# Two attention and feed-forward layers on one core: products with v leave the chip unnormalised, rows are divided per unit

## Chip, core and metric

The kernel runs on one core of a Trainium2 chip. Its engines are TensorE (PE, with PEld for its weight loads), VectorE (DVE), ScalarE (ACT), GpSimd (POOL) and SyncE (SP, which issues most transfers); sixteen DMA engines move the data. The metric is the device time of one execution in microseconds, less is better, told as the median of several runs.

## What is computed

The input is x, 2048 rows of 640 numbers in f32. Two layers are run with the same weights, each an attention block and a feed-forward block with layer normalisation in front and the input added behind:

```python
H = 32; Dh = D // H; W = 256            # D = 640, Dh = 20
q, k, v = split(layernorm(x) @ wqkv)    # 32 heads of 20
scores = q @ k.T * Dh ** -0.5           # key not after the query, under 256 rows back
x = x + concat_heads(softmax(scores) @ v) @ wo
h = relu(layernorm(x) @ w1 + b1) ** 2   # F = 1536
x = x + h @ w2 + b2
```

## The kernel before

**Units.** The rows are cut into units of T = 256 rows, eight a layer, so that the two layers make NU = 16 units (u = 0 to 15; u = 8 begins the second layer). A unit sees its own keys and those of the unit before. Numbers that enter dense products are held as two f16 tiles, a high part and what the rounding left, and `mm3` (L149) makes each product of three f16 products.

**Attention of a unit.** The 32 heads are handled in NQ = 8 quads of four. `max_quad` (PE L313, DVE L327) makes masked scores and their row maxima; `max_out` transposes four quads' maxima on PE (L335), splits them (L338, L339) and writes them by SP transfers (L346) into two spare rows of the q tile, so that the later score product already subtracts them. `exp_quad` makes the scores again (L365), takes exponentials on ACT (L372) and masks them on POOL (L383, L387). `pv_quad` multiplies with v (L412). Each head's v has a 21st column of the constant 1/64, so row 20 of each head's product is the sum of its exponentials, scaled. Before the change `pv_quad` then divides at once: the product is copied from PSUM on ACT (L423), transposed in 32x32 blocks on DVE (L426), the sums are inverted (L428), spread by a second transpose (L429), multiplied on POOL (L430), and split into f16 high and low parts (L433, L434). After every second quad four SP transfers (L438) write both parts to a DRAM tile `o`, 20 rows for each head.

**Dense stages.** `stage_qk` makes q (j = 0) and k (j = 1), five chunks of 128 columns each, copied out by ACT L243 and DVE L244, and sends them through DRAM (L249, L251, L259) into another layout. `stage_v` follows (L271). `load_o(u)` brings the attention output back (L450) and loads the rows of x to be added (L454). `stage_o` multiplies by wo, adds x (L465) and normalises the result. `y_cross` transposes by DMA (L217), `stage_y` on PE (L173). `stage_f` is the feed-forward block (L500 to L520). All accumulators, the transposes and the product with v share two PSUM buffers of the tag "mm".

**Order.** PE's order is the order of the program text; the other engines' orders are chosen by a planner. Generators yield a modelled cost in ns after each piece, and `together` runs a unit's quads and hands out pieces of the `dense` generator between them: a `share` of a modelled `cost` is spread evenly over the unit's quads, and with `whole` the rest is run at the unit's end. Maxima are made LEAD = 5 quads ahead of the exponentials. During unit u the dense work is q and k of u + 1, output product of u - 1, v of u + 1, feed-forward of u - 1. Unit 0 has q, k, v of unit 2 instead (a fifth of it is left for unit 1), units 1 and 15 have no projection of a next unit, and behind unit 15 come its output product and feed-forward as a tail. `load_o(u - 1)` is issued in unit u behind the scores of its first quad. The weights wo, w1 and w2 are loaded during units 0 and before (`load_w`, `late`): ACT issues each transfer (L118), makes the high part (L122), scales the rest (L124), and POOL makes the low part (L125).

## Time and profile before

| | us |
|---|---|
| median of three runs | 1797.43 |
| the three runs | 1800.69, 1797.43, 1793.38 |
| profiled execution | 1793.71 |
| its span | 1792.0 |

| engine | busy us | share of the span |
|---|---|---|
| PE | 1616.1 | 90% |
| PEld | 1177.0 | 66% |
| DVE | 1068.6 | 60% |
| ACT | 781.2 | 44% |
| POOL | 742.0 | 41% |

Times inside the profile count from the start of the span. L12 is line 12 of the kernel. An engine's idle time is put down to the instruction that ended it. A group of instructions is shown as line, engine, operation, output and input with their sizes, count, busy time and mean duration. Of the chain of waits that ended last, followed back from the end, 53% lie on PE, 19% on DVE, 8% on issuing, 8% on POOL, 6% on ACT and 5% on transfers. The mean granted clock of PE is 0.979.

### The profile page before, as it was taken

The numbers are of one execution on the slowest core, as the hardware profiler recorded it, in microseconds if no ns is written. First come the engines' busy times: TensorE is split into PE (matmuls) and PEld (weight loads), VectorE is DVE, ScalarE is ACT, GpSimd is POOL, SyncE is SP. The second block draws the span as 40 slices with busy tenths as digits, with TensorE's granted clock in tenths as the row PEclk, the third lists the DMA queues.
The fourth block names the chain that finished last, engine by engine and source line by source line (L and its number), as shares of the span: only waits on it lengthen the run. The fifth ranks groups of instructions, "written<-read, shape, count | busy, mean of one in ns | idle before, by whom it ended". The sixth has DMA issues, their size and how long they took to land.

```text
span 1792.0 us, 45770 instructions
## 1 busy us (share of the span) xinstructions
PE 1616.1 (90%) x17542; PEld 1177.0 (66%) x17542; DVE 1068.6 (60%) x3473; ACT 781.2 (44%) x1716; POOL 742.0 (41%) x1434
## 2 busy tenths in 40 slices
PE   5767798999999999999999999999999999998798
PEld 4544566676667766666777767667676767775567
DVE  6546465666666566666557665666656566564531
ACT  5464343444445344444535244453534435352522
POOL 4354343534435353443525244352534435353522
PEclk9889899999999999999999999999999999998999
DMA  6754103234161422515242432514143152511010
GB/s 207 182 162 115 39 24 109 59 90 112 35 141 46 119 65 76 126 35 139 48 131 57 112 86 63 135 38 126 46 108 90 53 131 45 134 27 61 17 37 30
DMA packets 239067, 154.90 MB, mean 86 GB/s; under 512 B 80640, under 2 KB 219776, under 8 KB 238848
## 3 DMA queue, kind: packets, MB, share of 16 engines
q1 hardware_dynamic: 230432, 142.46, 31.9%
q10 hardware_dynamic: 8416, 9.51, 1.9%
q8 instruction: 138, 2.26, 0.5%
q14 instruction: 81, 0.66, 0.1%
HBM read 82.58 MB, written 52.43 MB: 75 GB/s over the span
## 4 chain that ended last, share of the span: by engine, by line
PE 53%; DVE 19%; issue 8%; POOL 8%; ACT 6%; DMA 5%; SPq 1%; ACTq 0%; DVEq 0%; POOLq 0%
PE acc L149 41%; DVE bb L327 8%; PE pv L412 4%; ACT pt L372 4%; PE bb L365 3%; DVE mx L327 3%; PE bb L313 3%; POOL pt L387 2%; POOL pt L383 2%; DVE hh L505 2%; POOL r L503 2%; DMA qk<-qd 1%; DVE rb L426 1%; POOL po L430 1%; DVE qd L244 1%
## 5 line engine op out<-in xcount | busy, mean ns | idle before, releaser
L327 DVE CUSTOM_DVE_ANT_0 bb<-bb,maskb 128x384 f32<-128x384 f32 (+2 forms) x1024 | 512.6, 558 | 126.4 <-PE bb L313 125.3
L372 ACT ACTIVATE pt<-bb 128x512 f32<-128x512 f32 x736 | 372.1, 600 | 64.9 <-PE bb L365 63.9
L430 POOL TENSOR_TENSOR po<-po,rb 128x256 f32<-128x256 f32 x128 | 101.1, 790 | 651.2 <-DVE rb L429 544.8
L149 PE MATMUL acc<-y,w_s 128*128 128x256 f16 x2880 | 337.4, 275 | 13.5 <-ACT r L500 8.5
L149 PEld LDWEIGHTS <-w_s 128*128 128x128 f16 x2880 | 278.1, 98 | 75.0 <-issue 38.6
L149 PE MATMUL acc<-w_s,hh 128*128 128x320 f16 x2304 | 325.7, 299 | 0.0
L149 PE MATMUL acc<-yT,wq_s 128*128 128x256 f16 x2400 | 286.5, 278 | 14.8 <-DVE qd L244 9.8
L149 PEld LDWEIGHTS <-hh 128*128 128x128 f16 x2304 | 222.0, 98 | 97.0 <-issue 14.5
L149 PEld LDWEIGHTS <-wq_s 128*128 128x128 f16 x2400 | 233.9, 100 | 67.1 <-issue 35.9
L383 POOL TENSOR_SCALAR_AFFINE_SELECT pt<-pt 128x256 f32<-128x256 f32 x448 | 194.8, 443 | 100.4 <-ACT pt L372 89.0
L423 ACT COPY po<-pv 128x256 f32<-128x256 f32 x128 | 47.6, 372 | 379.3 <-PE pv L412 376.4
L412 PE MATMUL pv<-pt,vt 128*32 128x128 f32 (+1 forms) x3840 | 194.2, 332 | 20.1 <-ACT r L500 10.5
L387 POOL TENSOR_SCALAR_AFFINE_SELECT pt<-pt 128x256 f32<-128x256 f32 x512 | 202.4, 418 | 9.5 <-ACT pt L372 8.7
L505 DVE TENSOR_TENSOR hh<-r,hh 128x256 f16<-128x256 f32 x192 | 93.6, 499 | 137.0 <-ACT hh L504 133.2
L149 PE MATMUL acc<-wo_s,od 128*128 128x320 f16 x960 | 143.2, 305 | 32.4 <-DMA od<-o 17.0
L503 POOL TENSOR_TENSOR r<-r 128x256 f32<-128x256 f32 x192 | 116.9, 625 | 115.5 <-ACT r L500 114.3
L149 PE MATMUL acc<-wq_s,yT 128*128 128x320 f16 x960 | 142.9, 300 | 16.3 <-DVE mT L339 14.7
L412 PEld LDWEIGHTS pv<-pt,vt 128*32 128x32 f32 x3840 | 107.9, 110 | 70.9 <-issue 28.2
L433 ACT CAST ot<-po 128x256 f16<-128x256 f32 x128 | 52.3, 408 | 228.9 <-POOL po L430 228.9
L149 PEld LDWEIGHTS <-od 128*128 128x128 f16 x960 | 92.5, 99 | 81.2 <-issue 28.0
L327 DVE DVE_READ_ACCUMULATOR2_ANT mx<- 128x1 f32 x1024 | 143.6, 140 | 0.0
L365 PE MATMUL bb<-qt,kt 62*128 62x128 f16 (+1 forms) x1920 | 108.3, 246 | 27.9 <-DVE mx L327 20.2
(62 smaller groups left out, 1408.0 us busy)
## 6 DMA issues: line engine op xcount, KB each, us to landing
qk<-qd SPq DMA_DIRECT2D x32, 640.0 KB
qt<-qk SPq DMA_DIRECT2D x32, 480.0 KB
kt<-qk SPq DMA_DIRECT2D x32, 480.0 KB
qk<-qd SPq DMA_DIRECT2D x32, 320.0 KB
o<-ot SPq DMA_DIRECT2D x256, 40.0 KB
od<-o SPq DMA_DIRECT2D x32, 320.0 KB
stg<-in_B_w_dram ACTq DMA_DIRECT2D x30, 256.0 KB
xt<-in_A_x_dram SPq DMA_DIRECT2D x16, 320.0 KB
```

The costliest lines, as they stand in the source:

```text
L149: nc.tensor.matmul(acc, lhs(a, c), rhs(b, c), start=(k == 0), stop=(k == 3 * nk - 1))
L313: apart(nc.tensor.matmul(to, qt[r, p, i * P:(i + 1) * P], kt[r, p, a:b], start=True, stop=True), read)
L327: read.append(nc.vector.tensor_tensor_reduce(out=v, in0=v, in1=mask, scale=1.0, scalar=-3.0e38, op0=ALU.add, op1=ALU.max, accum_out=accum))
L365: apart(nc.tensor.matmul(bb[e][:, k, o:o + w], kt[r, 2 * qd + j, ko:ko + P], qt[r, 2 * qd + j, q0 * P:q0 * P + w], start=True, stop=True), ...
L372: at[0] = nc.scalar.activation(pt[:, :o], bb[e][:, k, :o], AF.Exp, scale=SCALE / (QS * QS))
L383: nc.gpsimd.affine_select(out=m, in_=m, pattern=[[0, 2], [-1, P]], compare_op=ALU.is_gt, fill=0.0, base=0, channel_multiplier=1)
L387: nc.gpsimd.affine_select(out=m, in_=m, pattern=[[0, 2], [1, P]], compare_op=ALU.is_ge, fill=0.0, base=0, channel_multiplier=-1)
L412: nc.tensor.matmul(pv[32 * jj:32 * (jj + 1), q0 * P:(q0 + qn) * P], vf[:, c:c + 32], pj[:, j, :], start=(k == 0), stop=(k == len(steps) - ...
L430: nc.gpsimd.tensor_tensor(po, po, rb.rearrange("p a b -> p (a b)"), op=ALU.mult)
L433: nc.scalar.copy(oh, pf)
L503: nc.gpsimd.tensor_tensor(r, r, r, op=ALU.mult)
L505: nc.vector.tensor_sub(hh[:, 1, f0 + f, :], r, hh[:, 0, f0 + f, :])
```

## The change

- `pv_quad` copies the product with its row of sums from PSUM into an f32 tile and does nothing more with it; that tile is written to DRAM, 21 rows a head. The DRAM tile has the order (21, head, row).
- `load_o` loads a unit's 640 value rows as five chunks of 128 partitions, partition d * 32 + head, chunk c for the numbers 4 c + d of each head, and the 32 rows of sums four times over, so that all 128 partitions have theirs. The new `norm_o` inverts the sums once (128x256), multiplies, and splits into high and low parts, one half of 128 rows after the other.
- Since the rows of `o` come in another order, the rows of wo are loaded in that order as well, one transfer a chunk.
- `norm_o` stands in the order of work in the second half of `stage_qk` (the hook) in units 2 to 14, ahead of the rest of the projection of unit 2 in unit 1, behind half of the carried work in unit 15, and behind 6 us of modelled work in the tail. In unit 15 and in the tail other tiles are used for the loaded output.
- Unit 0 takes 0.7 instead of 0.8 of the projection of unit 2. Unit 14 leaves 9 us of modelled dense work (CARRY) to unit 15, whose share becomes 0.65 instead of 0.6. The tail runs 6 us and 4 us of modelled work ahead of its output product instead of 8 us.
- The maxima are kept in another order, so that the 256 columns of both halves go in one transfer for each of two spare rows and two head halves: four transfers instead of eight.

```diff
--- before.py
+++ after.py
@@ -115,8 +115,14 @@
         m = c1 - c0
         sv = st[:, :m * n].rearrange("p (c n) -> p c n", c=m)
         with behind(at[0] if late else None):
-            (nc.scalar if late else nc.sync).dma_start(
-                sv, src[c0 * P:c1 * P, lo:lo + n].rearrange("(c p) n -> p c n", p=P))
+            if dst is wo_s:
+
+                v = src.rearrange("(h c d) n -> c d h n", c=KC, d=4)
+                for c in range(c0, c1):
+                    nc.scalar.dma_start(sv[:, c - c0], v[c, :, :, lo:lo + n])
+            else:
+                (nc.scalar if late else nc.sync).dma_start(
+                    sv, src[c0 * P:c1 * P, lo:lo + n].rearrange("(c p) n -> p c n", p=P))
         hi = dst[:, 0, c0:c1, lo:lo + n]
         low = dst[:, 1, c0:c1, lo:lo + n]
         nc.scalar.activation(hi, sv, AF.Copy, scale=WS)
@@ -224,7 +230,7 @@
 
     held = []
 
-    def stage_qk(u, hold=False):
+    def stage_qk(u, hold=False, hook=None):
         yT = yTs[u]
         qt = sb.tile([P, NP, T], F16, name="qt", tag="qt", bufs=2)
         kt = kts[u % 3]
@@ -233,6 +239,8 @@
             qd = sb.tile([P, KC, 2, T], F16, name="qd", tag="qd", bufs=1)
             for c0 in range(0, KC, 2):
                 n = min(2, KC - c0)
+                if hook and j and c0 == 2:
+                    hook()
                 acc = ps.tile([P, 2, T], F32, name="acc", tag="mm", bufs=2)
                 for c in range(n):
                     lo = j * D + (c0 + c) * P
@@ -291,7 +299,7 @@
         qt, cur, prev = qts[u], kts[u % 3], kts[(u - 1) % 3]
         G = qd // GQ
         if (u, G) not in mxs:
-            mxs[u, G] = sb.tile([P, 2, 2, 2 * GQ], F32, name="mx", bufs=2)
+            mxs[u, G] = sb.tile([P, 2, 2 * GQ, 2], F32, name="mx", bufs=2)
         mx = mxs[u, G]
         bb = banks()
 
@@ -315,7 +323,7 @@
             now = []
             for e in range(2):
                 s0 = p % (2 * GQ)
-                accum = mx[:, i, e, s0:s0 + 1]
+                accum = mx[:, e, s0, i:i + 1]
                 if w == 3:
                     now.append((bb[e][:, o // P:, 3 * P:], maskb[:, o:].rearrange("p (a n) -> p a n", n=P), accum))
                 else:
@@ -332,19 +340,17 @@
         qt, mx = qts[u], mxs.pop((u, G))
         NR = 8 * GQ
         tr = ps.tile([P, 4, P], F32, name="tr", tag="mm", bufs=2)
-        nc.tensor.transpose(tr[:NR, 0, :], mx.rearrange("p i e n -> p (i e n)"), ident)
+        nc.tensor.transpose(tr[:NR, 0, :], mx.rearrange("p e n i -> p (e n i)"), ident)
         mT = sb.tile([NR, 2, P], F16, name="mT", bufs=1)
         with first():
             nc.vector.tensor_scalar(mT[:, 0], tr[:NR, 0, :], -1.0 / MS, None, op0=ALU.mult)
             nc.vector.scalar_tensor_tensor(mT[:, 1], tr[:NR, 0, :], -1.0 / MS, mT[:, 0],
                                            op0=ALU.mult, op1=ALU.subtract)
-        for i in range(2):
-            for e in range(2):
-                s0 = (2 * i + e) * 2 * GQ
-                for a in range(2):
-                    r = 64 * e + 3 * DH + a
-                    nc.sync.dma_start(qt[r:r + 1, 2 * GQ * G:2 * GQ * (G + 1), i * P:(i + 1) * P],
-                                      mT[s0:s0 + 2 * GQ, a, :])
+        for e in range(2):
+            for a in range(2):
+                r = 64 * e + 3 * DH + a
+                nc.sync.dma_start(qt[r:r + 1, 2 * GQ * G:2 * GQ * (G + 1), :].rearrange("p n (i m) -> p (n i) m", i=2),
+                                  mT[4 * GQ * e:4 * GQ * (e + 1), a, :])
 
     ods, ots = {}, {}
 
@@ -414,53 +420,64 @@
                                              stop=(k == len(steps) - 1), skip_group_check=True,
                                              tile_position=(0, 32 * jj))
         if qd == 0:
-            ods[u] = tc.dram_tile([D, 2, 2, P], F16, name=f"o{u}")
+            ods[u] = tc.dram_tile([DH + 1, H, T], F32, name=f"o{u}")
         if qd % 2 == 0:
-            ots[u] = sb.tile([P, 2, 2, 2, P], F16, name="ot", bufs=1)
-        ot, dr = ots[u], ods[u]
-        po = sb.tile([P, T], F32, name="po", bufs=2)
+            ots[u] = sb.tile([P, 2, T], F32, name="ot", bufs=2)
+        ot = ots[u]
         with first():
-            nc.scalar.copy(po, pv)
-
-        rb = sb.tile([P, T // 32, 32], F32, name="rb", bufs=1)
-        nc.vector.transpose(rb.rearrange("p a b -> p (a b)"), po)
-        rc = sb.tile([P, T // 32, 1], F32, name="rc", bufs=1)
-        nc.vector.reciprocal(rc, rb[:, :, DH:DH + 1])
-        nc.vector.transpose(rb.rearrange("p a b -> p (a b)"), rc.to_broadcast([P, T // 32, 32]))
-        nc.gpsimd.tensor_tensor(po, po, rb.rearrange("p a b -> p (a b)"), op=ALU.mult)
-        oh, ol = ot[:, qd % 2, :, 0, :], ot[:, qd % 2, :, 1, :]
-        pf = po.rearrange("p (i n) -> p i n", i=2)
-        nc.scalar.copy(oh, pf)
-        nc.vector.tensor_sub(ol, pf, oh)
+            nc.scalar.copy(ot[:, qd % 2], pv)
         if qd % 2:
-            drv = dr.rearrange("(q j d) i a n -> j d q (i a n)", j=4, d=DH)
+            drv = ods[u].rearrange("d (q j) n -> j d q n", j=4)
             for j in range(4):
-                nc.sync.dma_start(drv[j][:, qd - 1:qd + 1, :],
-                                  ot[32 * j:32 * j + DH].rearrange("p q i a n -> p q (i a n)"))
+                nc.sync.dma_start(drv[j][:, qd - 1:qd + 1, :], ot[32 * j:32 * j + DH + 1])
 
     x1s, ys, y2s = {}, {}, {}
 
     ols = {}
 
-    def load_o(u, tag="hh", xtag="x1"):
+    def load_o(u, late=False):
 
         l, g = divmod(u, NG)
-        od = sb.tile([P, 2, KC, 2, P], F16, name="od", tag=tag, bufs=1)
-        for i in range(2):
-            nc.sync.dma_start(od[:, i].rearrange("p c a n -> p c (a n)"),
-                              ods[u].rearrange("(c p) i a n -> i p c (a n)", p=P)[i])
-            x1 = sb.tile([P, D], F32, name="x1", tag=xtag, bufs=2)
+        if late:
+            val = sb.tile([P, KC, T], F32, name="ov", tag="qt", bufs=2)
+            od = sb.tile([P, KC, 2, T], F16, name="od", tag="yT", bufs=1)
+        else:
+            raw = sb.tile([P, 2, KC, T], F32, name="od", tag="hh", bufs=1)
+            val = raw[:, 0]
+            od = raw[:, 1].rearrange("p c n -> p (c n)").bitcast(F16).rearrange("p (c a n) -> p c a n", a=2, n=T)
+        rs = sb.tile([P, T], F32, name="rs", bufs=1)
+        nc.sync.dma_start(val, ods[u][:DH].rearrange("(c d) h n -> (d h) c n", d=4))
+        nc.sync.dma_start(rs, ods[u][DH:].to_broadcast([4, H, T]))
+        if u == NU - 1:
+            both = sb.tile([P, 2, D], F32, name="x1", tag="qt", bufs=2)
+            x1 = [both[:, i] for i in range(2)]
+        else:
+            x1 = [sb.tile([P, D], F32, name="x1", bufs=2) for i in range(2)]
+        for i in range(2):
             with behind(trip[0]):
-                nc.sync.dma_start(x1, xsrc(l, 2 * g + i))
-            ols[u, i] = od[:, i], x1
+                nc.sync.dma_start(x1[i], xsrc(l, 2 * g + i))
+        ols[u] = val, od, rs, x1
+
+    def norm_o(u):
+
+        val, od, rs, x1 = ols[u]
+        nc.vector.reciprocal(rs, rs)
+        for i in range(2):
+            q = slice(i * P, (i + 1) * P)
+            nc.vector.tensor_tensor(val[:, :, q], val[:, :, q], rs[:, q].unsqueeze(1).to_broadcast([P, KC, P]),
+                                    op=ALU.mult)
+            nc.scalar.copy(od[:, :, 0, q], val[:, :, q])
+            nc.vector.tensor_sub(od[:, :, 1, q], val[:, :, q], od[:, :, 0, q])
+        return iter(())
 
     def stage_o(u):
-        for i in range(2):
-            od, x1 = ols.pop((u, i))
+        _, od, _, x1b = ols.pop(u)
+        for i in range(2):
+            x1 = x1b[i]
             for h in range(2):
                 acc = ps.tile([P, 2, T], F32, name="acc", tag="mm", bufs=2).rearrange("p a n -> p (a n)")
                 hs = slice(h * HD, (h + 1) * HD)
-                yield from mm3(acc[:, :HD], lambda a, k: od[:, k, a, :], lambda c, k: wo_s[:, c, k, hs], KC, 136)
+                yield from mm3(acc[:, :HD], lambda a, k: od[:, k, a, i * P:(i + 1) * P], lambda c, k: wo_s[:, c, k, hs], KC, 136)
                 with first():
                     nc.vector.scalar_tensor_tensor(x1[:, hs], acc[:, :HD], 1.0 / (OS * WS), x1[:, hs],
                                                    op0=ALU.mult, op1=ALU.add)
@@ -544,6 +561,14 @@
         for m in todo:
             yield 1.0, None, m
 
+    def some(dense, cost):
+        while cost > 0:
+            c = next(dense, None)
+            if c is None:
+                break
+            cost -= c
+            yield c
+
     def upto(dense, cost):
         while cost > 0:
             c = next(dense, None)
@@ -589,7 +614,7 @@
         if whole:
             run(dense)
 
-    QKC, VC, OC, FCST, LNC = 16.4e3, 8.2e3, 8.2e3, 39.2e3, 1.2e3
+    QKC, VC, OC, FCST, LNC, CARRY = 16.4e3, 8.2e3, 8.2e3, 39.2e3, 1.2e3, 9e3
 
     order = tc.manual_schedule(engines={mybir.EngineType.PE})
     ctx.enter_context(order)
@@ -620,26 +645,31 @@
 
             ln_load(3)
             rest = chain(stage_qk(2, True), stage_v(2), ln_t(3))
-            together(quads, ahead[NQ - LEAD:], rest, QKC + VC + LNC, 0.8, False, later)
+            together(quads, ahead[NQ - LEAD:], rest, QKC + VC + LNC, 0.7, False, later)
             run(later)
             continue
         parts, cost, ahead_ln = [], OC + FCST, None
+        norm = lambda: norm_o(u - 1)
         if 1 < u < NU - 1:
-            parts += [stage_qk(u + 1), stage_o(u - 1), lambda: (y_cross(u - 1), iter(()))[1], stage_v(u + 1)]
+            parts += [stage_qk(u + 1, hook=norm), stage_o(u - 1), lambda: (y_cross(u - 1), iter(()))[1], stage_v(u + 1)]
             cost += QKC + VC
             if u + 2 < NU:
                 ahead_ln = u + 2
+        elif u == 1:
+            upto(rest, 5e3)
+            parts += [norm, rest, stage_o(0), stage_y(0)]
+            cost += LNC + 0.3 * (QKC + VC + LNC) - 5e3
         else:
-            parts += [rest] * (u == 1) + [stage_o(u - 1), stage_y(u - 1)]
-            cost += LNC + (u == 1) * 0.2 * (QKC + VC + LNC)
-        if u == 1:
-            upto(rest, 5e3)
-        f = stage_f(u - 1, ahead_ln)
-        dense = chain(*parts, f)
-        together(quads, ahead, dense, cost, 0.6 if last else 1.0, not last, after=lambda: load_o(u - 1), pace=NQ)
-    load_o(NU - 1, "yT", "qt")
-
-    upto(dense, 8e3)
+
+            parts += [some(dense, 0.5 * CARRY), norm, dense, stage_o(u - 1), stage_y(u - 1)]
+            cost += LNC + CARRY
+        dense = chain(*parts, stage_f(u - 1, ahead_ln))
+        share = 0.65 if last else 1.0 - CARRY / cost if u == NU - 2 else 1.0
+        together(quads, ahead, dense, cost, share, u < NU - 2, after=lambda: load_o(u - 1, last), pace=NQ)
+    load_o(NU - 1, True)
+    upto(dense, 6e3)
+    norm_o(NU - 1)
+    upto(dense, 4e3)
     run(stage_o(NU - 1))
     run(dense)
     run(stage_y(NU - 1), stage_f(NU - 1))
```

## The prediction, made before the result was known

> **What bounds the kernel now.** I read first how busy each engine is in stretches cut at the starts of the units (each row: stretch, its length, then busy time of PE, PEld, DVE, ACT, POOL, the granted clock, DMA share, GB/s). The stretches are: up to unit 1's q and k; unit 0's attention; unit 1; units 2 to 13; unit 14; unit 15 (the tail, 1714 to 1792, is left out).
>
> ```profile
> 0.00:59.34 59.34, 32.85 (x240) 24.68 (x241) 29.68 (x73) 29.46 (x60) 23.94 (x32) 0.96 0.77 215
> 59.34:177.73 118.39, 88.20 (x811) 58.77 (x810) 70.64 (x283) 63.98 (x137) 54.55 (x74) 0.88 0.52 142
> 177.73:281.00 103.27, 83.12 (x927) 57.73 (x926) 58.25 (x199) 40.80 (x93) 42.02 (x88) 0.90 0.13 34
> 281.00:1533.07 1252.07, 1183.58 (x13233) 871.17 (x13234) 793.25 (x2567) 549.61 (x1209) 526.00 (x1049) 1.00 0.36 87
> 1533.07:1629.00 95.93, 91.67 (x1035) 68.27 (x1036) 56.74 (x183) 44.94 (x99) 41.53 (x87) 1.00 0.32 81
> 1629.00:1714.22 85.22, 66.05 (x758) 42.93 (x756) 40.78 (x127) 38.46 (x88) 40.71 (x86) 0.90 0.13 36
> ```
>
> In the middle (281 to 1629, thirteen units) PE is busy 1275 of 1348 us: it is the bound, and the change takes no matmul away. What can be gained is PE's idle time: 73 us there, and 57 + 20 + 19 us in the start, unit 1 and unit 15, where the clock is also down. So next I read what ends PE's waits: first of units 2 to 14, then the od row of unit 1, then two rows of unit 15 (total us, times, longest).
>
> ```profile
> PE acc L149 <- DVE qd L244: 21.6, 26, 1.1
> PE acc L149 <- DVE mT L339: 14.7, 12, 1.5
> ...
> PE bb L365 <- DVE mx L327: 10.2, 13, 0.9
> ...
> PE bb L365 <- DVE rc L428: 2.8, 9, 0.8
> PE acc L149 <- DMA y<-yl: 2.8, 3, 1.2
> ...
> PE acc L149 <- DMA od<-o: 9.3, 1, 9.3
> ...
> PE acc L149 <- DMA od<-o: 7.5, 1, 7.5
> PE pv L412 <- POOL pt L387: 5.0, 3, 2.1
> ```
>
> The reader is to see two things. In the middle, 49 of the 73 us (21.6 + 14.7 + 10.2 + 2.8) are ended by DVE, in many waits of about 1 us: DVE is not full (63%), but works in bursts. At units 1 and 15 one long wait stands for the attention output to come back from DRAM.
>
> **The change, part by part: DVE, ACT and POOL.** These groups hold the removed operations and the nearest relatives of the new ones (busy us, mean ns of one, idle before).
>
> ```profile
> L430 POOL TENSOR_TENSOR po<-po,rb 128x256 f32<-128x256 f32 x128 | 101.1, 790 | 651.2 <-DVE rb L429 544.8 <-DVE bmv L163 86.3 <-ACT pt L372 11.9
> ...
> L434 DVE TENSOR_TENSOR ot<-po,ot 128x256 f16<-128x256 f32 x128 | 58.5, 457 | 93.7 <-ACT ot L433 93.7
> L429 DVE STREAM_TRANSPOSE rb<-rc 128x256 f32<-128x256 f32 x128 | 56.5, 442 | 3.2
> L426 DVE STREAM_TRANSPOSE rb<-po 128x256 f32<-128x256 f32 x128 | 56.3, 440 | 7.7 <-ACT po L423 7.7
> ...
> L433 ACT CAST ot<-po 128x256 f16<-128x256 f32 x128 | 52.3, 408 | 228.9 <-POOL po L430 228.9
> L215 DVE TENSOR_TENSOR yl<-xt,yl 128x640 f16<-128x640 f32 x50 | 50.0, 1018 | 19.8 <-ACT yl L214 19.8
> ...
> L214 ACT CAST yl<-xt 128x640 f16<-128x640 f32 x50 | 35.3, 732 | 15.6 <-PE acc L149 15.6
> ...
> L428 DVE RECIPROCAL rc<-rb 128x8 f32<-128x8 f32 x128 | 25.3, 198 | 0.5
> ...
> L164 DVE TENSOR_SCALAR bmv<-bmv 128x1 f32<-128x1 f32 x64 | 9.1, 143 | 1.3
> ```
>
> Removed per unit (eight quads): DVE 8 x (440 + 198 + 442 + 457) = 12.3 us, POOL 8 x 0.79 = 6.3 us, ACT 8 x 0.41 = 3.3 us. The copy of pv stays as it is; it only writes to the f32 tile that leaves.
>
> Added per unit: two subtractions of 640 elements, 2 x 1.02 on DVE (L215 has this shape); two multiplications of 640, bounded by the 0.5 us of a 256-element one (L434) and L215's 1.02, taken at 1.0; two ACT copies, 2 x 0.73 (L214); one reciprocal of 128x256, which no row shows. Its lower bound is that of any 256-element pass (0.44, L426). The upper one takes the small reciprocal's excess over a one-element operation as a price per element: (198 - 143) / 8 = 6.9 ns, times 256 plus 143 is 1.9 us. I take 1.9, since L428 is the same operation. DVE: 1.9 + 2.0 + 2.0 = 5.9 added against 12.3 removed, 6.4 us a unit less (of 66); ACT 1.8 less, POOL 6.3 less. The transfers stay in number: sixteen writes of o a unit, now of 21 rows, and two loads, 640 KB and 128 KB, for the two of 320 KB; the SP queue gets no longer. None of this is on PE, so it counts only where DVE's bursts make PE wait. One such wait in unit 6 (start, duration, operation, idle before):
>
> ```profile
> 713.18 0.44 DVE L426 STREAM_TRANSPOSE rb<-po 128x256 f32<-128x256 f32 x1
> ...
> 714.00 0.20 DVE L428 RECIPROCAL rc<-rb 128x8 f32<-128x8 f32 x1
> 714.12 0.64 DVE L244 SCALAR_TENSOR_TENSOR qd<-acc,qd 128x512 f16<-128x512 f32 x1
> ...
> 714.81 1.25 PE L149 MATMUL acc<-yT,wq_s 128*128 128x256 f16 x10 [0.63 <-DVE qd L244]
> ```
>
> L426 and L428 stand in the burst ahead of L244, which frees PE's accumulator; together about 0.5 us of the 0.63 us wait. So I let half of the qd waits go (11), 0.5 us of each of the 13 mx waits (6.5) and the rc waits (2.8): 20 us gross. The mT waits stay: maxima alone stand ahead of them. Against it, the new block of 5.9 us is placed in the second half of the q and k stage, ahead of two evacuations a unit; I charge 0.8 us a unit, about one 640-element pass, 10 us. **Middle: -10 us**, bounds 0 and -24 (the gross, and the y row and rest besides); the bound above zero is the rival below.
>
> **Rows of maxima.** Eight transfers per half unit become four of twice the rows, and the transpose on PE is the same size.
>
> ```profile
> 744.68 2.79 SPq L346 DMA_DIRECT2D qt<-mT  x4
> ```
>
> That is 0.7 us of SP's queue each, 5.6 us a unit less. SP's queue is passed by the transposed y, for which PE waited 2.8 us in all; the maxima themselves are made five quads ahead. At most -3 us, inside the middle's bound; I count nothing.
>
> **Units 0 and 1.** A tenth of unit 2's q, k, v work (2.6 us) moves behind unit 0. Unit 1's output product waited for this:
>
> ```profile
> 169.74 0.37 ACT L423 COPY po<-pv 128x256 f32<-128x256 f32 x1 [3.05 <-PE pv L412]
> ...
> 175.27 4.09 SPq L438 DMA_DIRECT2D o<-ot  x4
> ...
> 183.74 0.96 SPq L450 DMA_DIRECT2D od<-o  x2
> ...
> 187.01 6.34 PE L149 MATMUL acc<-wo_s,od 128*128 128x320 f16 x30 [9.28 <-DMA od<-o]
> ```
>
> Now the rows can leave at 170.1 instead of 175.3, but the division follows the load: reciprocal, first half's multiplication, copy and subtraction, 1.9 + 1.0 + 0.7 + 1.0 = 4.6 us ahead of the first matmul. Write 8.5 us and load 3.3 as here: 170.1 + 11.8 + 4.6 = 186.5. With the 3.7 us (1636.40 to 1640.08) and 3.2 us of unit 15 (next fence): 181.6. So 0.5 to 5.4 us earlier; the moved work fills the wait without shortening the sum unless unit 0 shrinks, where PE idles 30 us and DVE loses 12 us of work. **-5 us together**, bounds +1 and -9.
>
> **Unit 15 and the tail.** Up to 9 us of unit 14's dense work is carried into unit 15 and stands ahead of the output product. The chain there, and the clock in the two 5 us stretches at and behind it:
>
> ```profile
> 1636.40 0.30 SPq L438
> ...
> 1640.08 3.18 DMA od<-o
> ...
> 1640.00:1645.00 5.00, 1.70 (x7) 1.01 (x8) 0.00 (x0) 0.00 (x0) 0.00 (x0) 0.50 0.67 200
> 1645.00:1650.00 5.00, 5.00 (x60) 2.91 (x58) 2.45 (x9) 0.00 (x0) 0.00 (x0) 0.62 0.00 0
> ```
>
> The wait of 7.5 us ends at 1643.3; the new chain, starting from a copy about 4 us earlier but with 4.6 us of division, ends near the same time, and 9 us of carried work now lies over it. After the wait PE ran 1.7 us at half clock and 5 us at 0.62: (1.7 x 0.5 + 5 x 0.38) = 2.7 us more. **-10 us**; bounds -14 (some of POOL's 5.0 goes too) and -4 (the cover reaches half). If the cover were gone, 7.5 us would be back.
>
> ```profile
> 1714.28 0.37 ACT L423 COPY po<-pv 128x256 f32<-128x256 f32 x1 [1.18 <-PE pv L412]
> ...
> 1718.38 1.42 SPq L438 DMA_DIRECT2D o<-ot  x4
> ```
>
> In the tail the chain loses the steps between the copy's end and the first write (3.7 us) and gains 4.6 of division and one more load; the cover ahead grows from 8 to 10 us. **+1**, bounds -1 and +3.
>
> **The loads of wo.** Seven transfers become ten, each of 128 rows taken 4 x 32 with a stride.
>
> ```profile
> L122 ACT ACTIVATE wo_s<-stg 128x512 f16<-128x512 f32 x6 | 3.8, 629 | 11.1 <-DMA stg<-in_A_wo_dram 11.1
> ...
> 38.17 3.78 DMA stg<-in_A_wo_dram
> ```
>
> ACT stands still for these loads (11.1 us for six), and one lies on the chain of waits, since the accumulators of unit 0 are copied out behind it on ACT; the q and k of unit 1 wait for that. Bytes and row lengths are as before, so the low bound is 0; if every load took twice as long, ACT would lose another 11 us, the high bound. I take **+5**.
>
> The page "DMA: Bandwidth & Descriptors" of the Trainium skill (section on why a DMA increments its semaphore by 16) says a transfer runs on at most as many engines as divide the slowest dimension of both sides; with 4 outermost, a wo load would use 4 of 16 engines. By it the sum would be 6 us higher; no row before has such a transfer. The loads of the row sums have the same form, but come well ahead of their use.
>
> **Sum.** 5 - 5 - 10 - 10 + 1 = -19 on the profiled execution's 1793.7 (its span of 1792.0 and 1.7 around it): 1774.7. That execution lies 3.7 under the median of the three runs; I put the forecast between, at 1776.
>
> **The rivals.**
> *Slow start.* Four engines carry each wo load. In the first stretch 215 GB/s at a share of 0.77 is 17 GB/s for each engine: 262 KB takes 3.8 us on four, 0.95 on sixteen, 2.9 us more, and about four such loads follow one another behind ACT's waits: +11 instead of +5, 1782. For: the trace has ACT waiting for each of them. Against: part of the start waits elsewhere (57 us of PE idle with many releasers). The page of the Trainium skill named above speaks for it.
> *The stall moves on.* DVE's bursts are mostly maxima; freed time is filled by the next instruction and PE waits for it instead. The middle gives 0: 1786. For: 14.7 us are mT's, with none of the removed work ahead. Against: the unit 6 rows.
> *Slower: DVE blocked by the division.* The reciprocal or the copy between multiplication and subtraction holds DVE's in-order queue: 5.9 us in one piece, or longer while ACT is at its exponentials. PE has two accumulators, 30 products each, about 3.5 us (10 in 1.25 us in the unit 6 rows); a block longer than that makes L244 late and PE stops. 5.9 + 1.0 - 3.5 = 3.4 us in each of 13 units is +44, less the 20 gross: +24 in place of -10, 1810. For: today's copy and subtraction wait for each other (93.7 us at L434). Against: a unit is 1252 / 12 = 104 us; the load is issued at its start and the hook comes 0.7 of the q and k stage later, 104 x 0.7 x 16.4 / 72 = 17 us, against 7 us for write and load; and evacuations have priority.
> *It doesn't do what it says:* carried work runs out before the division is done, so both long waits stay: -10 and -5 become 0, 1791.
>
> **Chances.** Forecast 0.49, slow start 0.18, stall moves on 0.15, slower 0.12, no cover 0.06. This kernel can be told from no change at about 0.5%, 1788 to 1806. Nearly all of the first two and 0.1 of the third lie under 1788: faster 0.75; same 0.13 (rest of the third, the last, spill); slower 0.12. Range 1757 (middle -24, ends at their bounds in part) to 1804 (no cover with a slow start); above it is the blocked DVE, below it little. The likeliest's own is 1760 to 1789.
>
> **What would show it.** Right: no od wait over 2 us in units 1 and 15, clock near 1.00 there; qd and rc waits of PE halved in units 2 to 14, DVE at 57% there; the new reciprocal near 1.9 us. Wrong: PE waits of 2 us or more for qd behind the 640-element operations; wo waits on ACT over 20 us and unit 1's first q matmul much after 59 us; a long wait for the divided od in the tail.

## The result and the profile after

| | us | ratio to before, 95% interval |
|---|---|---|
| before, median of 7 | 1794.98 (1789.14 to 1800.69) | |
| after, median of 7 | 1804.19 (1799.83 to 1807.81) | 1.005, 1.0029 to 1.0071 |
| span profiled, before / after | 1792.0 / 1803.6 | |

Of all executions of the kernels below, one, of e11, took 3212 us; it enters no ratio.

The change makes the kernel 0.5% slower; 1776 was forecast, and the range ended at 1804. The first part of the page of after (busy time, share and instructions of each engine) shows that the work did go away:

```profile
PE 1632.8 (91%) x17542; PEld 1185.7 (66%) x17542; DVE 975.7 (54%) x3041; ACT 760.7 (42%) x1620; POOL 631.2 (35%) x1306
```

DVE has 93 us less to do, POOL 111, ACT 20. PE has the same products and is busy 17 us longer.

To find the place I cut both traces at the same PE instructions: the first q product of unit 1, and the first product with wo for units 0, 1 and 13. Columns as in the prediction: stretch, length, busy time of PE, PEld, DVE, ACT, POOL, granted clock, DMA share, GB/s. The stretches are start; unit 0; unit 1; middle; unit 15 and tail. After:

```profile
0.00:73.87 73.87, 37.09 (x240) 26.84 (x241) 30.21 (x73) 29.75 (x61) 24.58 (x32) 0.90 0.61 172
73.87:201.90 128.03, 90.50 (x811) 60.17 (x811) 62.65 (x255) 64.39 (x136) 51.64 (x74) 0.83 0.54 145
201.90:313.90 112.00, 103.74 (x1190) 73.58 (x1191) 65.33 (x211) 47.31 (x101) 38.56 (x88) 0.95 0.18 49
313.90:1574.30 1260.40, 1198.00 (x13248) 879.38 (x13248) 726.86 (x2244) 534.85 (x1137) 440.40 (x953) 0.98 0.36 88
1574.30:1803.60 229.30, 203.48 (x2055) 145.70 (x2053) 90.67 (x261) 84.35 (x188) 76.07 (x160) 0.97 0.15 44
```

Before, cut likewise (its start is the first row of the prediction, 59.34):

```profile
59.34:187.01 127.67, 88.20 (x811) 58.77 (x810) 71.02 (x283) 66.67 (x142) 57.57 (x82) 0.86 0.54 143
187.01:306.10 119.09, 106.48 (x1191) 76.06 (x1192) 71.04 (x241) 47.94 (x107) 45.95 (x97) 0.92 0.16 44
306.10:1557.00 1250.90, 1182.40 (x13233) 870.67 (x13233) 793.69 (x2569) 550.02 (x1208) 525.85 (x1048) 1.00 0.36 87
1557.00:1792.00 235.00, 206.13 (x2069) 146.81 (x2068) 103.19 (x310) 87.07 (x199) 88.68 (x175) 0.96 0.16 42
```

The prediction cut the middle and unit 15 at the starts of units, these rows cut at the output products; the stretches answer to each other.

| stretch | predicted | measured |
|---|---|---|
| start | +5 | +14.5 |
| units 0 and 1 | -5 | +0.4 - 7.1 = -6.7 |
| middle | -10 | +9.5 |
| unit 15 and tail | -9 | -5.7 |
| sum | -19 | +11.6 |

Two terms fail: the start by size, the middle by sign. In the middle PE's idle time did not grow: 1250.90 - 1182.40 = 68.5 us before, 1260.40 - 1198.00 = 62.4 after. Its busy time for the same products grew by 15.6 us, and the granted clock fell from 1.00 to 0.98. So the next view is what the waits are made of, here in after (the engine that waits, what ends the wait; total us, times, longest): first of the whole execution, then of PE in the middle, then in unit 15 and the tail:

```profile
DVE rs L464 <- DMA rs<-o: 65.3, 16, 8.0
ACT wo_s L128 <- DMA stg<-in_A_wo_dram: 28.8, 7, 7.5
PE acc L155 <- ACT od L469: 9.8, 1, 9.8
...
PE pv L418 <- DVE qd L252: 33.9, 13, 4.1
...
PE acc L155 <- DVE qd L252: 9.1, 12, 0.8
...
PE bb L371 <- DVE mx L335: 8.8, 3, 8.1
```

DVE stands still 65.3 us for the row sums, once for each of the 16 units. Before, PE waited for q and k in many short pieces (21.6 us in 26, none over 1.1). Now there are 12 of these left (9.1 us) and 13 longer ones at the products with v: twelve of 2.2 to 4.1 us, one in each of the units 3 to 14, and one of 1.6. Unit 6 has the second longest. Its timeline in after (start, duration, engine, line; a queue's name ends in q; in brackets the idle time before and what ended it):

```profile
703.39 1.51 PE L418 MATMUL pv<-pt,vt 128*32 128x256 f32 x32
...
708.85 0.49 DVE L534 SCALAR_TENSOR_TENSOR x<-acc,x 128x320 f32<-128x320 f32 x1 [1.34 <-PE acc L155]
708.97 0.60 SPq L450 DMA_DIRECT2D rs<-o  x1
...
712.93 1.75 DVE L464 RECIPROCAL rs<-rs 128x256 f32<-128x256 f32 x1 [3.59 <-DMA rs<-o]
715.30 1.56 DVE L467 TENSOR_TENSOR od<-od,rs 128x640 f32<-128x640 f32 x2 [0.62 <-DMA od<-o]
716.92 1.56 DVE L470 TENSOR_TENSOR od<-od 128x640 f16<-128x640 f32 x2
...
718.40 0.68 DVE L252 SCALAR_TENSOR_TENSOR qd<-acc,qd 128x512 f16<-128x512 f32 x1
719.23 2.79 PE L418 MATMUL pv<-pt,vt 128*32 128x256 f32 x32 [3.32 <-DVE qd L252]
```

Read it downwards. The load of the sums is issued at 708.97. The next thing in DVE's queue is already the reciprocal; DVE waits 3.59 us for the sums, then runs the whole block, and the copy-out of q or k (L252), which frees PE's accumulator, comes behind all of it. PE waits 3.32 us and then needs 2.79 us for the 32 products that took 1.51 at 703.39. The stretches around this place give the clock (the column after POOL):

```profile
715.00:718.00 3.00, 0.91 (x20) 0.59 (x18) 2.64 (x4) 1.83 (x3) 0.00 (x0) 1.00 0.33 97
718.00:721.00 3.00, 1.77 (x28) 1.40 (x32) 3.00 (x9) 0.12 (x1) 0.00 (x0) 0.50 0.06 23
721.00:724.00 3.00, 3.00 (x22) 1.62 (x15) 2.22 (x10) 0.37 (x1) 0.00 (x0) 0.50 0.02 5
724.00:727.00 3.00, 3.00 (x26) 2.51 (x24) 1.00 (x2) 0.98 (x2) 0.00 (x0) 0.86 0.00 0
```

In this wait of 3.3 us the clock fell to a half, and PE ran on at that for some 5.5 us. The other waits cost about as much or less: of the twelve long ones ten are followed by a lower clock, while after those of 2.39 us (at 825.62) and 2.20 us (at 926.95) it stayed at 1.00. In the whole middle the products with v are busy 155.5 us against 144.4 before; that is 11.1 of the 15.6 us by which PE's busy time grew. The groups of the new operations in after (busy us, mean ns, idle before) show that the new work was priced well, a little too high:

```profile
L464 DVE RECIPROCAL rs<-rs 128x256 f32<-128x256 f32 x16 | 28.0, 1753 | 65.3 <-DMA rs<-o 65.3
L467 DVE TENSOR_TENSOR od<-od,rs 128x640 f32<-128x640 f32 x28 | 21.8, 821 | 2.6 <-DMA od<-o 2.2
```

### The profile page after: what moved, and what is told of

Same layout as the page of the kernel before. It is cut to its first block, busy times and chain, and to the rows that moved or that the text cites. A ratio compares the mean times of both kernels' runs of the same rounds, so it can differ in the third digit from the quotient of the medians.

```text
span 1803.6 us, 44320 instructions
## 1 busy us (share of the span) xinstructions
PE 1632.8 (91%) x17542; PEld 1185.7 (66%) x17542; DVE 975.7 (54%) x3041; ACT 760.7 (42%) x1620; POOL 631.2 (35%) x1306
## 5 line engine op out<-in xcount | busy, mean ns | idle before, releaser
L389 POOL TENSOR_SCALAR_AFFINE_SELECT pt<-pt 128x256 f32<-128x256 f32 x448 | 186.2, 421 | 627.5 <-ACT pt L378 615.5
L155 PE MATMUL acc<-y,w_s 128*128 128x256 f16 x2880 | 333.5, 275 | 2.4 <-DVE y L182 2.2
L155 PE MATMUL acc<-yT,wq_s 128*128 128x256 f16 x2400 | 296.4, 285 | 9.7 <-DVE qd L252 5.3
L155 PEld LDWEIGHTS <-wq_s 128*128 128x128 f16 x2400 | 239.0, 102 | 69.5 <-issue 33.5
L418 PE MATMUL pv<-pt,vt 128*32 128x128 f32 (+1 forms) x3840 | 204.5, 344 | 56.3 <-DVE qd L252 36.6
L393 POOL TENSOR_SCALAR_AFFINE_SELECT pt<-pt 128x256 f32<-128x256 f32 x512 | 206.8, 427 | 60.3 <-ACT pt L378 59.3
L428 ACT COPY ot<-pv 128x256 f32<-128x256 f32 x128 | 47.5, 371 | 376.4 <-PE pv L418 376.4
L522 DVE TENSOR_TENSOR hh<-r,hh 128x256 f16<-128x256 f32 x192 | 84.2, 449 | 181.1 <-ACT hh L521 174.8
L252 DVE SCALAR_TENSOR_TENSOR qd<-acc,qd 128x512 f16<-128x512 f32 (+1 forms) x96 | 56.4, 598 | 140.9 <-ACT qd L251 140.9
L155 PEld LDWEIGHTS <-yT 128*128 128x128 f16 x960 | 93.1, 99 | 50.4 <-issue 15.5
```

Source lines behind the costliest of these rows:

```text
L155: nc.tensor.matmul(acc, lhs(a, c), rhs(b, c), start=(k == 0), stop=(k == 3 * nk - 1))
L252: nc.vector.scalar_tensor_tensor(qd[:, c0:c0 + n, 1, :], acc[:, :n, :], s, qd[:, c0:c0 + n, 0, :], op0=ALU.mult, op1=ALU.subtract)
L389: nc.gpsimd.affine_select(out=m, in_=m, pattern=[[0, 2], [-1, P]], compare_op=ALU.is_gt, fill=0.0, base=0, channel_multiplier=1)
L393: nc.gpsimd.affine_select(out=m, in_=m, pattern=[[0, 2], [1, P]], compare_op=ALU.is_ge, fill=0.0, base=0, channel_multiplier=-1)
L418: nc.tensor.matmul(pv[32 * jj:32 * (jj + 1), q0 * P:(q0 + qn) * P], vf[:, c:c + 32], pj[:, j, :], start=(k == 0), stop=(k == len(steps) - ...
L428: nc.scalar.copy(ot[:, qd % 2], pv)
```

## The experiments

The theory: the start is lost to wo loads that run on few DMA engines, and the middle to a reciprocal that stands at the head of DVE's in-order queue before its sums have landed. Rivals: the work of the block itself, the form of the sums' load, the transfers of maxima. Each kernel's time is a median, and its ratio is to the kernel before, run again beside it; "start" is the first q product of unit 1 in its profiled execution. In e1, e7, e9 and e10 the rows of wo stand in another order than those of the attention output, so they serve for their times alone.

| kernel | us | ratio, 95% interval | start |
|---|---|---|---|
| e1_wo_plain | 1792.0 | 0.9969, 0.9948 to 0.9989 | 61.29 |
| e2_rs_four | 1813.13 | 1.0095, 1.0072 to 1.0118 | 73.69 |
| e3_hd | 1783.8 | 0.9924, 0.9904 to 0.9943 | 62.56 |
| e4_behind | 1782.15 | 0.9913, 0.9895 to 0.9932 | 74.89 |
| e5_hd_behind | 1760.1 | 0.9808, 0.9794 to 0.9823 | 62.12 |
| e6_before_max4 | 1793.26 | 0.9995, 0.9983 to 1.0008 | 61.48 |
| e7_before_wo4 | 1809.09 | 1.0082, 1.0067 to 1.0097 | 74.20 |
| e8_no_carry | 1765.26 | 0.9844, 0.9829 to 0.9859 | 63.01 |
| e9_before_wo8 | 1805.95 | 1.0047, 1.0032 to 1.0062 | 65.09 |
| e10_before_wo2 | 1828.7 | 1.0172, 1.0121 to 1.0224 | 90.78 |
| e11_after_u15 | 1803.09 | 1.0036, 1.0022 to 1.0049 | 74.26 |
| e12_all | 1759.24 | 0.9777, 0.9757 to 0.9797 | 62.52 |

### The start: e1, e7, e9, e10

e1 is the changed kernel with the plain wo loads:

```diff
-            if dst is wo_s:
-                v = src.rearrange("(h c d) n -> c d h n", c=KC, d=4)
...
+            (nc.scalar if late else nc.sync).dma_start(
+                sv, src[c0 * P:c1 * P, lo:lo + n].rearrange("(c p) n -> p c n", p=P))
```

> The changed kernel with wo loaded by the seven transfers of the kernel before (its rows then stand in another order than the attention output, so the output differs). If the late start is the strided wo loads, the first product of unit 1's q moves from 73.9 back to about 59.5 us, ACT's waits for wo fall from 28.8 to about 13.6 us, and the whole goes from 1804 to about 1790. If the start is late for another reason (the planner's other order, the other loads), it stays past 70 us and the time at 1804.

e7 is the kernel before with the strided loads alone; e9 and e10 are e7 with another outermost count:

```diff
-                v = src.rearrange("(h c d) n -> c d h n", c=KC, d=4)
+                v = src.rearrange("(h c d) n -> c d h n", c=KC, d=8)   # e9; d=2 in e10
```

> The kernel before with only the wo loads of the change, 4 x 32 rows a transfer (wo's rows then stand in another order than the attention output, so the output differs). If this edit alone makes the start late, unit 1's first q product comes at 72 to 75 us instead of 59.3 and the whole is 11 to 15 us slower. If the start was late only together with the planner's other order in the changed kernel, under 4 us slower.

> The kernel before with the wo loads in ten transfers of 8 x 16 rows instead of 4 x 32 (wo's rows in another order than the attention output, so the output differs). If a transfer moves on as many DMA engines as its outermost dimension counts, the first lone wo load shows a DMA share near 0.5, lands in about 3.5 us instead of 4.8, and unit 1's first q product comes at 65 to 68 us, between 59.3 and 74.2. If the stride is what costs, it stays at 72 to 75 us.

> The kernel before with the wo loads as 2 x 64 rows (the output differs as above). By the count of the outermost dimension: a share near 0.13 during the first lone load, which takes about 8 us, and unit 1's first q product at 88 to 105 us. By the stride: 72 to 75 us again.

e1 brings the start back to 61.29 and ACT's waits for wo from 28.8 to 14.3 us; e6, further on, which leaves the start as it was before, has 61.48, so no delay is left. The edit of e7 alone makes the start 74.20 and costs 0.8%. The first wo load runs alone (in after the bytes of the 1 us stretches from 28 to 32 us add up to the 262 KB of this one load), so its share of the 16 DMA engines can be read. After, e9 and e10, each with one 1 us stretch during that load, in after and e9 the one with the highest share, and the row of ACT that waits for it:

```profile
30.00:31.00 1.00, 1.00 (x12) 0.90 (x10) 0.00 (x0) 0.00 (x0) 0.00 (x0) 1.00 0.27 104
...
32.21 0.63 ACT L128 ACTIVATE wo_s<-stg 128x512 f16<-128x512 f32 x1 [4.80 <-DMA stg<-in_A_wo_dram]
```

```profile
29.00:30.00 1.00, 1.00 (x12) 0.89 (x10) 0.00 (x0) 0.00 (x0) 0.00 (x0) 1.00 0.44 172
...
30.61 0.63 ACT L128 ACTIVATE wo_s<-stg 128x512 f16<-128x512 f32 x1 [3.65 <-DMA stg<-in_A_wo_dram]
```

```profile
30.00:31.00 1.00, 1.00 (x12) 0.89 (x11) 0.00 (x0) 0.00 (x0) 0.00 (x0) 1.00 0.13 41
...
34.42 0.63 ACT L128 ACTIVATE wo_s<-stg 128x512 f16<-128x512 f32 x1 [7.22 <-DMA stg<-in_A_wo_dram]
```

Outermost counts of 4, 8 and 2 give shares of 0.27, 0.44 and 0.13, that is close to 4, 8 and 2 of 16 engines, and the start follows in that order: 73.87, 65.09, 90.78. The rule of the Trainium skill that the prediction weighed (page "DMA: Bandwidth & Descriptors", section "Why a DMA increments its semaphore by 16 and not by 1") takes the largest number of engines, up to 16, that divides the slowest dimension of both sides. These runs agree with it.

### The layout: e2, e3

e2 is the changed kernel with the sums in four transfers of 32 rows each; e3 puts the 32 heads outermost everywhere:

```diff
-        nc.sync.dma_start(rs, ods[u][DH:].to_broadcast([4, H, T]))
+        for d in range(4):                                              # e2
+            nc.sync.dma_start(rs[d * H:(d + 1) * H], ods[u][DH])
```

```diff
-                v = src.rearrange("(h c d) n -> c d h n", c=KC, d=4)
+                v = src.rearrange("(h c d) n -> c h d n", c=KC, d=4)    # e3
...
-        nc.sync.dma_start(val, ods[u][:DH].rearrange("(c d) h n -> (d h) c n", d=4))
-        nc.sync.dma_start(rs, ods[u][DH:].to_broadcast([4, H, T]))
+        for c in range(KC):
+            nc.sync.dma_start(val[:, c], ods[u][4 * c:4 * c + 4].rearrange("d h n -> h d n"))
+        nc.sync.dma_start(rs, ods[u][DH].unsqueeze(1).to_broadcast([H, 4, T]))
```

> The changed kernel with the row sums loaded by four transfers of 32 rows each instead of one with 4 outermost. If that transfer is slow because it runs on four engines, DVE's waits for it fall from 65 us to under 30, PE's waits for qd from 58 us to under 35, the tail's load from 6.4 to about 3.5 us, and the time falls by 8 to 15 us. If DVE waits because its queue reaches the division before any load can be back, the waits stay above 50 us and the time within 4 us.

> Both transfers with 32 outermost (partition head * 4 + d in place of d * 32 + head; the values then need five transfers a unit instead of one). If the number outermost is what makes both slow, the start returns to about 60 us and DVE's waits for the sums fall under 30 us: 1778 to 1786, faster than the kernel before. If strides and the three further wo transfers are the cause, the start stays past 70 us and the time above 1795; bytes, row lengths and the number of wo transfers are those of the changed kernel.

e2 is a miss: it lost time, which neither of the two expectations had. In its timeline of unit 6 the four pieces do not go out together:

```profile
709.72 1.23 SPq L451 DMA_DIRECT2D rs<-o  x2
711.05 0.39 SPq L449 DMA_DIRECT2D od<-o  x1
...
712.06 0.90 SPq L451 DMA_DIRECT2D rs<-o  x2
...
717.21 1.75 DVE L465 RECIPROCAL rs<-rs 128x256 f32<-128x256 f32 x1 [6.69 <-DMA rs<-o]
```

The load of the 640 KB of values is issued between the pieces, and DVE stands 6.69 us instead of 3.59; that this order is the reason was not tried. In the whole execution DVE stands 102.1 us for the sums instead of 65.3, and the middle, cut as above, takes 1270.1 us.

e3 repairs the start (62.56). In the tail its sums land 2.6 us after the issue instead of 6.4, but there the values go out well ahead, where in after they go out 0.4 us ahead. Its waits of DVE only change name: 25.2 us for the sums and 36.1 for the values, 61 against 65. The middle takes 1256.0 us, only 4.4 less than in after, while e1 and e11, which have the middle of after, take 1257.6 and 1257.8. So in the middle it is hardly the load's form that decides, but that DVE stands there at all. Nor is the clock the whole loss: in the middle of e3 it is 1.00 and PE is busy 1185.9 us, yet the stretch is nearly as long, with more idle time.

### The reciprocal's place: e4, e5

The same block, with the reciprocal put in DVE's queue behind the last copy-out of q or k that the program has ahead of it. No wait is taken away, only the order is changed; e5 is e3 and e4 together.

```diff
+                    out_at[0] = nc.vector.scalar_tensor_tensor(qd[:, c0:c0 + n, 1, :], ...)   # in stage_qk
...
-        nc.vector.reciprocal(rs, rs)
+        with behind(out_at[0]):
+            nc.vector.reciprocal(rs, rs)
```

> The changed kernel with the reciprocal queued on DVE behind the last copy-out of q and k ahead of the hook; transfers as in the change. If the middle loses because DVE's queue stands at the reciprocal too early, DVE's waits for the sums in units 2 to 14 go to nearly 0, PE's qd waits fall under 25 us, and the time falls by 10 to 20 us, with start and tail as they were. If the block of division itself (5.5 us in one piece) is what holds PE, PE's waits stay within a quarter of 73 us in all that DVE ends and the time within 4 us of 1804.

> Both repairs at once: 32 outermost in the wo and sum loads, and the reciprocal queued behind a copy-out of q and k. If the late start and DVE's standing at the reciprocal are two separate losses, their gains add: start as with 32 outermost (62.6 us), middle as with the queued reciprocal, 1766 to 1772, 1.3 to 1.7% under the kernel before. If they overlap, about 1780, as each alone.

The middle of e4 by stretches, and unit 6 in its timeline:

```profile
313.00:1550.50 1237.50, 1187.67 (x13248) 872.74 (x13248) 723.85 (x2252) 535.30 (x1139) 442.94 (x955) 1.00 0.37 89
...
718.54 0.69 DVE L253 SCALAR_TENSOR_TENSOR qd<-acc,qd 128x512 f16<-128x512 f32 x1 [4.75 <-ACT qd L252]
719.15 1.74 DVE L466 RECIPROCAL rs<-rs 128x256 f32<-128x256 f32 x1
```

The copy-out goes first, the reciprocal finds its sums there, and the clock is 1.00 again. The middle takes 1237.5 us: 22.9 less than after with all the block's work still in it, and 13.4 less than before. DVE's waits for sums fall from 65.3 to 19.4 us, in units 1 and 15 and the tail, where no copy-out of q or k is near. With the loads of e3 the same edit does the same: the middle falls from 1256.0 to 1234.8 us in e5. The gains of e3 and e4 add up: e5 takes 1760.1, under the 1766 to 1772 expected and 1.9% less than before.

### Parts alone: e6, e8

e6 is the kernel before with the four transfers of maxima; e8 is e5 without the carried work:

```diff
-    QKC, VC, OC, FCST, LNC, CARRY = 16.4e3, 8.2e3, 8.2e3, 39.2e3, 1.2e3, 9e3
+    QKC, VC, OC, FCST, LNC, CARRY = 16.4e3, 8.2e3, 8.2e3, 39.2e3, 1.2e3, 0.0    # e8; share 0.6, whole up to unit 14
```

> The kernel before with only the rows of maxima in four transfers instead of eight. If SP's queue was on no path that sets the end, within 4 us of the kernel before; if the shorter queue lets transposed rows and maxima through earlier, 4 to 10 us faster, in units 2 to 14.

> The twice repaired kernel without the work carried from unit 14 into unit 15 (share 0.6 again). If the carried work covers the wait for the divided output, the wait at unit 15's output product comes back, 7 to 12 us of PE idle with its half clock, and the kernel is 6 to 12 us slower than with it. If the chain had become short enough without, within 3 us.

The maxima make no difference, as counted. Without the carried work e5 is 5.2 us slower, a little under what was expected. The waits of PE in e8 show a second wait for the divided output beside the one of unit 1, that of unit 15, and it is the longer one:

```profile
PE acc L155 <- ACT od L472: 17.6, 2, 9.3
```

### Unit 15: e11, e12

In after, PE has no wait for od in unit 15, but the one of 8.1 us for maxima. Its timeline, DVE and SP, then PE:

```profile
1641.81 0.48 DVE L534 SCALAR_TENSOR_TENSOR x<-acc,x 128x320 f32<-128x320 f32 x1
1644.38 0.61 SPq L450 DMA_DIRECT2D rs<-o  x1
1650.26 1.75 DVE L464 RECIPROCAL rs<-rs 128x256 f32<-128x256 f32 x1 [7.97 <-DMA rs<-o]
...
1658.90 1.95 PE L371 MATMUL bb<-qt,kt 62*128 62x256 f16 x16 [8.12 <-DVE mx L335]
```

DVE stood from 1642.3, even before the load was issued, with the maxima that PE waits for behind the reciprocal. e11 is the changed kernel with the reciprocal of this unit put behind the last block of maxima ahead of it in the program; e12 is e5 with the same edit.

```diff
+                max_at[0] = read[-1]                                    # in max_quad
...
-        nc.vector.reciprocal(rs, rs)
+        with behind(max_at[0] if u == NU - 2 else None):
+            nc.vector.reciprocal(rs, rs)
```

> The changed kernel with one edit: in unit 15 the reciprocal is put behind the last block of row maxima that the program text has ahead of it on VectorE (eight maxima and one copy-out of an accumulator now run before it); nothing else moves. Theory (the reciprocal at the head of VectorE's queue took the place of the od wait in unit 15): in the changed kernel VectorE stands 7.97 us for the sums there and PE waits 8.1 us for maxima, then runs 1.95 and 4.2 us where 0.83 and 2.9 do, 2.4 us more. Then the wait of PE for mx of 8.1 us goes and the time falls by 6 to 10 us, to about 1796 (ratio to the kernel before 1.000 plus or minus 0.002), and no od wait over 2 us appears, since the output product starts 17 us after the reciprocal. Rival (the wait only moves: the output product, or the exponentials behind POOL, then wait as long): within 2 us of the changed kernel, 1802 to 1806, with a wait for od of 5 us or more in unit 15.

> The kernel with both repairs (head-major loads, reciprocal behind the last q or k copy-out) plus the same edit for unit 15. Theory: there VectorE stood 1.0 us and PE 5.1 + 0.9 us for maxima in unit 15, partly for the exponentials and not for the sums, so less is to be had: 2 to 5 us, about 1756 (ratio 0.977 to 0.980). Rival (the 5.1 us wait belongs to the exponentials alone, which the reciprocal does not hold up): no difference from 1760, ratio 0.980 to 0.982.

Unit 15 (from the output product in unit 14 to the one in unit 15) in e11, the same with the tail, and its reciprocal:

```profile
1571.30:1656.40 85.10, 83.14 (x960) 58.17 (x959) 50.67 (x162) 40.29 (x88) 37.92 (x80) 1.00 0.24 60
1571.30:1790.90 219.60, 200.57 (x2055) 144.10 (x2053) 91.02 (x261) 84.20 (x188) 78.48 (x160) 1.00 0.17 46
...
1648.07 1.74 DVE L467 RECIPROCAL rs<-rs 128x256 f32<-128x256 f32 x1
```

The wait is gone and no od wait takes its place: that stretch falls from 93.9 us in after (1574.3 to 1668.2) to 85.1, and with the tail from 229.3 to 219.6. In its ratio e11 shows less of this: 1.0036 against 1.005 for after, some 2.5 us, with intervals that overlap, and its median lies where the rival was expected. Its profiled execution took 1792.5 us at a mean clock of 0.970, the ones that were timed lie at 1801 to 1804 at 0.964 to 0.968. So the mechanism is seen, but its size in e11's time stays open. For e12 against e5 the two measures differ: the ratios, 0.9777 against 0.9808, make 5.5 us, a little more than the theory said, with intervals that just meet; the medians, 1759.24 and 1760.1, make 0.9 us, which is the rival's. So this size stays open as well.

## Why the prediction was wrong, and where it was right

**The start (+5, measured +14.5): mis-sized.** The step that failed is "I take +5". The mechanism was named as a rival at +11, and set aside because the start waits for many things. ACT's waits for wo grew by 28.8 - 13.6 = 15.2 us, and the start by 14.5: nearly all of it passes through. e1, e7, e9 and e10 show that the outermost count of these loads is the cause.

**The middle (-10, measured +9.5): wrong sign.** In the sum the step that failed is "I charge 0.8 us a unit": in each unit PE paid a wait of 2.2 to 4.1 us for the copy-out of q or k, and often a lower clock behind it. It rests on the "against" of the slower rival, which failed with it: "the load is issued at its start and the hook comes 0.7 of the q and k stage later", 17 us, enough for write and load. That is the order of the program text, and only PE follows it. DVE's order is the planner's, and there the reciprocal stood next: in unit 6 DVE had nothing ahead of it from 709.34 (708.85 + 0.49), 0.4 us after the load began to be issued. That the loads of the sums "come well ahead of their use" falls with it. That rival named the right engine and queue, but priced the wrong part of it (+24): it counted the block as 5.9 us in one piece, where it was 5.0 (1.75 + 2 x 0.82 + 2 x 0.82), and e4 keeps all of it without the loss. What cost was the standing for the sums ahead of the block: 22.9 us between after and e4, 21.2 between e3 and e5.

**What the removed work is worth.** With the queue's order mended (e4) the middle is at -13.4, inside the predicted bounds of 0 and -24 and near the -10. That is in part luck: the sum came, most of its terms did not. These are waits of PE in the middle, one row of before and three of e4:

```profile
PE acc L149 <- DVE mT L339: 13.5, 11, 1.5
...
PE acc L155 <- DVE qd L253: 17.8, 22, 2.1
PE bb L372 <- DVE mx L336: 9.8, 14, 3.7
...
PE acc L155 <- ACT ot L429: 8.1, 10, 1.8
```

The waits for rc went, as counted. But those for q and k, of which half was to go, fell only from 21.0 to 19.3 us (1.5 of them at the products with v), and those for mx from 10.2 to 9.8. What went besides is the mT waits, 13.5 us, which the prediction kept, and most of those for ACT's part of the feed-forward block (17.7 to 3.4 us). New waits for the masks of POOL (1.2 to 8.7) and for the copy of pv (8.1) took some of it back. "Maxima alone stand ahead of them" was a misreading; in unit 6 of before, removed work stands between the two operations that make mT:

```profile
744.38 0.27 DVE L338 TENSOR_SCALAR mT<-tr 32x128 f16<-32x128 f32 x1
744.58 0.42 DVE L434 TENSOR_TENSOR ot<-po,ot 128x256 f16<-128x256 f32 x1
744.92 0.27 DVE L339 SCALAR_TENSOR_TENSOR mT<-tr,mT 32x128 f16<-32x128 f32 x1
...
745.25 0.97 PE L149 MATMUL acc<-wq_s,yT 128*128 128x320 f16 x6 [1.20 <-DVE mT L339]
```

**Units 0 and 1 (-5, measured -6.7): about right in size, not in its reasons.** The wait of unit 1 did not get shorter: 9.3 us for od before, 9.8 after, since the sums land late there too (of the wait from 192.1 to 201.9, 5.8 us lie before the reciprocal can start at 197.9, the rest is the division). The 7.1 us of unit 1 are 2.7 of PE's busy time, at a clock of 0.95 instead of 0.92, and 4.4 of idle time in other, shorter waits. Which edit brings that was not tried.

**Unit 15 and the tail (-9, measured -5.7).** "9 us of carried work now lies over it" holds for the od wait (e8 brings it back, 9.3 us), but the same reciprocal at the head of DVE's queue put an 8.1 us wait for maxima in its place. The cover that was counted for one engine was taken from another. With that removed, e11's profiled execution has -15.4 in this stretch (235.0 to 219.6).

**Small terms.** The reciprocal takes 1.75 us (1.9 taken), the 640-element operations 0.82 (1.0), the maxima's transfers change nothing (e6).

**The signs set beforehand.** Two of the three for "wrong" came: PE waits of 2 us and more for qd behind the 640-element operations (up to 4.1), and wo waits over 20 us with a late first q product. The third, a long wait for the divided od in the tail, did not: DVE stood 5.0 us there for the sums, and PE had no wait for od there.

## What to carry to other kernels

Moving work off the common path into one block was worth 13.4 us of the middle here, but an operation that waits for a transfer must be placed in its engine's own queue behind what others wait for: the program's order says nothing of a queue that a planner fills. Price a new wait by what it can do to PE's clock as well as by its length. And count the outermost dimension of a rearranged transfer before anything else: in these runs it set how many DMA engines carried it.

## What was not expected of the hardware

- One wait of 3.3 us was enough to leave PE at a granted clock of 0.50 for over 6 us (from 718 to between 724.5 and 725 in unit 6), while before's 68.5 us of idle time in the middle, in waits of at most 1.5 us, left it at 1.00. Length alone does not settle it: after waits of 2.22 to 2.64 us the clock fell seven times in the middle, after those of 2.20 and 2.39 it did not. Idle time fell by 6 us and the stage still got 9.5 us longer.
- A load of 256 KB with an outermost count of 2, 4 or 8 runs at a share of 0.13, 0.27 or 0.44 of the 16 engines; with 32 outermost (e3) the share was 0.71 in a 1 us stretch.
- With the division moved out of the quads, some unchanged operations got shorter: the subtraction of the feed-forward block (128x256, DVE) took 499 ns before and 449 after. In e6 and e7, which keep the division in place, it took 507 and 499. Which of the removed operations slowed it was not tried.
